# Linear attention into a gated feed-forward block: the third batch's projection and scores two slots later, a q load ahead of k and v, and the last additions in another order

## The chip, the core and the metric

The kernel runs on one core of a Trainium2 chip. The core has a matrix engine (TensorE, PE in the profile; its weight loads are PEld), a vector engine (VectorE, DVE), an engine for activations (ScalarE, ACT), a general one (GpSimd, POOL) and one that issues transfers (SyncE, SP). Sixteen DMA engines move data; loads are issued from POOL, stores and transposing transfers from SP. The metric is the device time of one launch in microseconds (us).

## The reference

Eight batches (b) with eight heads each. E and F project 1024 positions to 64 before the attention, and the result goes through a gated feed-forward block:

```python
k_proj = einsum('ks,bhsd->bhkd', E, k)          # k, v: 8 x 8 x 1024 x 64; E, F: 64 x 1024
v_proj = einsum('ks,bhsd->bhkd', F, v)
scores = (1 / sqrt(64)) * q @ k_proj.T          # per batch and head: 1024 x 64
attn   = exp(scores - max) / (sum(...) + 1e-9)
x      = (attn @ v_proj) laid out as 8192 x 512
g      = x @ w_gate                             # 512 x 1536
out    = (g * sigmoid(g) * (x @ w_val)) @ w_out # 1536 x 512
```

Inputs and output are float32; the kernel multiplies in bf16.

## The kernel before

**Chunks and iterations.** The 8192 rows are cut into 16 chunks of 512 (c; two to a batch, and chunk c belongs to batch c // 2). The feed-forward block takes 12 iterations to a chunk, one for each 128 of the 1536 columns: `f_g` (four matmuls with w_gate, then a tanh on ACT) and `f_v` (four with w_val, then two products on DVE, which make the bf16 tile hT). There are 192 iterations t.

**Slots.** Everything that the attention needs is put into numbered slots, two to an iteration. In iteration t the program order is: `f_g`, slot 2t, `f_v`, pieces of the output product of the chunk before (`f_m`), slot 2t + 1. Each engine works through its own instructions in this program order and waits at the first that isn't ready. The slots are written out by hand in `place(b)` and the lines behind it; in a slot, loads come first.

**Batches.** The text counts batches from 0, so the third batch is b == 2. For a batch the slots hold:

- `load_k`, `load_v`, and `load_q` twice (the two halves of 512 rows): DMAs from POOL's queue that convert float32 to bf16.
- `u_KV` (L162): sixteen matmuls in which k with E and v with F alternate; they use different halves of the array. ACT copies the k part (L170), DVE the v part into block-diagonal tiles (L174, L175).
- `u_KT` (L263): four matmuls that turn the projected k; DVE copies the result into block-diagonal tiles (L275, L276).
- `u_TD` (L331): a transposing DMA from SP's queue that turns one half of q into qTd.
- `u_S` (L353), eight of them: four matmuls of qTd with the projected k, an exponential on ACT; `u_R` one slot later sums and inverts on DVE; `u_N` (L383) multiplies on POOL and writes AAd.
- `u_AD` (L338): a transposing DMA from SP that turns AAd into AT; it waits for the four `u_N` of its half.
- `u_PV` (L410), eight: one matmul each of AT with the projected v; ACT copies the result to xT, which `f_g` and `f_v` of the chunk read.

Batch 1's slots: scores at 35 to 38 and 41 to 44, transpositions of weights at 41 and 47, products with v at 44, 45, 46, 46 and 66 to 69. POOL also computes sums of hT (L547, two to an iteration in the second half of a chunk) and sums for the output (L583, L594).

**The output product** of a chunk is made with fewer multiplications from sums and differences of quarters (a Strassen-like scheme with seven products m). For each half p of the rows, x holds products 3 and 5, 4 and 2; z holds 1 and 7, and 6. For the last chunk `f_m_last` does this without a next chunk to hide behind. Its products come in the order 3, 6, 4, 5 and 2, then 7, then 1. ACT copies x (`m_34`: xs; `m_52`: into ysb), POOL adds xs's halves into tt, and DVE does the rest. Products 7 and 1 of the same p use the same bank, so 1 has to wait until the addition behind 7 has read it. The four stores go out from SP (p = 0) and ACT (p = 1).

Of the kernel before, what the change touches and what calls it, by code (L numbers as in the profile page):

```python
# [10 lines left out]
ALU = mybir.AluOpType  # L11
# [27 lines left out]
def kernel(  # L39
# [19 lines left out]
    nc = tc.nc  # L59
# [450 lines left out]
    def rows_of(c):  # L510
        b, ch = divmod(c, CH)
        return out[b * S : (b + 1) * S, :].rearrange("(p c j) d -> p c j d", c=CH, j=4)[:, ch]
# [41 lines left out]
    def m_mm(c, p, m, ps, start=False):  # L554

        for f in range(HF):
            if m == 3:
                lhsT = hT[c][:, f, p * P : (p + 1) * P]
            elif m == 4:
                lhsT = hT[c][:, HF + f, HT + p * P : HT + (p + 1) * P]  # L560
            else:
                lhsT = hs[c, m][:, f, p * P : (p + 1) * P]
            rhs = {2: wo[:, f, 0:HC], 5: wo[:, HF + f, HC:DM]}.get(m)
            nc.tensor.matmul(  # L564
                out=ps,
                lhsT=lhsT,
                rhs=ws[m][:, f, :] if rhs is None else rhs,
                start=(start and f == 0),
                stop=(f == HF - 1),
                skip_group_check=True,  # L570
            )

    xx, zz, tt, yo = {}, {}, {}, {}

    def m_bank(at):
        return bank(at, [P, 2, HC], FP32, "yps")

    def m_34(c, p):

        xs = d_pool.tile([P, 2, HC], FP32, name="xs", tag="d")  # L580
        nc.scalar.copy(out=xs[:], in_=xx[c, p][:])  # L581
        t = tt[c, p] = d_pool.tile([P, 2, HC], FP32, name="tt", tag="t")
        nc.gpsimd.tensor_tensor(out=t[:, 0], in0=xs[:, 0], in1=xs[:, 1], op=ALU.add)  # L583

    def m_52(c, p):

        ysb = yo[c, p] = y_pool.tile([P, 4, HC], FP32, name="ysb", tag="ysb")
        nc.scalar.copy(out=ysb[:, 1:3], in_=xx.pop((c, p))[:])  # L588
# [27 lines left out]
    def f_m_last(c):  # L616

        xx[c, 0], xx[c, 1] = m_bank("y"), m_bank("g")
        z6 = m_bank("a")
        z1 = [m_bank("av"[p]) for p in range(2)]  # L620
        for p in range(2):
            m_mm(c, p, 3, xx[c, p][:, 0], start=True)
        for p in range(2):
            m_mm(c, p, 6, z6[:, p], start=(p == 0))
        for p in range(2):
            m_mm(c, p, 4, xx[c, p][:, 1])
            m_34(c, p)
        for p in range(2):
            m_mm(c, p, 5, xx[c, p][:, 0])
            m_mm(c, p, 2, xx[c, p][:, 1])  # L630
            m_52(c, p)
            d, ysb = tt[c, p], yo[c, p]
            nc.vector.tensor_tensor(out=d[:, 1], in0=d[:, 0], in1=ysb[:, 2], op=ALU.subtract)
            nc.vector.tensor_tensor(out=d[:, 0], in0=d[:, 0], in1=ysb[:, 1], op=ALU.subtract)
            nc.vector.tensor_tensor(out=d[:, 1], in0=d[:, 1], in1=z6[:, p], op=ALU.add)
        for x in (1, 0):
            for p in range(2):
                m_mm(c, p, (7, 1)[x], z1[p][:, 0], start=(x == 1))
                ysb = yo[c, p]
                nc.vector.tensor_tensor(out=ysb[:, 3 * x], in0=tt[c, p][:, x], in1=z1[p][:, 0], op=ALU.add)  # L640
                (nc.sync, nc.scalar)[p].dma_start(
                    out=rows_of(c)[:, p + 2 * x, :], in_=ysb[:, 2 * x : 2 * x + 2].rearrange("p x d -> p (x d)")
                )


    slots = defaultdict(list)

    def put(s, fn, *a):
        slots[s].append((fn, a))

    def place(b):
        s0 = 48 * (b - 1)
        if b == 1:
            put(22, u_TD, 1, 0)
            put(29, u_K1, 1)
            put(32, u_KT, 1)
            put(40, u_V1, 1)
            sa = (35, 36, 37, 38, 41, 42, 43, 44)
            put(41, u_AD, 1, 0)
            put(30, u_TD, 1, 1)  # L660
            put(47, u_AD, 1, 1)
            sp = (44, 45, 46, 46, 66, 67, 68, 69)
        else:
            put(s0 + (8 if b == 2 else 0), u_KV, b)
            put(s0 + (11 if b == 2 else 3), u_KT, b)
            o = 14 if b == 2 else 6
            put(s0 + (9 if b == 2 else -6), u_TD, b, 0)
            put(s0 + (11 if b == 2 else -4), u_TD, b, 1)
            sa = [s0 + o + 3 * j for j in range(NJ)]
            put(sa[3] + 4, u_AD, b, 0)  # L670
            put(sa[7] + 4, u_AD, b, 1)
            sp = [s0 + i for i in (39, 41, 43, 45, 57, 59, 61, 63)]
        for j in range(NJ):
            put(sa[j], u_S, b, j)
            put(sa[j] + 1, u_R, b, j)
            put(sa[j] + 1, u_N, b, j)
        for i in range(8):
            put(sp[i], u_PV, b, i // 4, i % 4)
# [5 lines left out]
    with tc.manual_schedule():  # L684
# [3 lines left out]
        for i in range(2):  # L688
            nc.scalar.dma_start(
                out=kraw[i][:],  # L690
                in_=k[0, 2 * i : 2 * i + 2].rearrange("h (p j) d -> p h (j d)", j=NJ),
# [123 lines left out]
        for b in range(1, B):  # L815
            place(b)
        for b in range(2, B):
            s0 = 48 * (b - 1) - (20 if b == 3 else 24)
            at = (43, 43, 44, 45) if b == 2 else (s0, s0 + 2, s0 + 4, s0 + 6)
            put(at[0], load_k, b)  # L820
            put(at[1], load_v, b)
            put(at[2], load_q, b, 0)
            put(at[3], load_q, b, 1)
# [25 lines left out]
        for t in range(NIT):  # L849
            c, f = divmod(t, NFT)  # L850
# [5 lines left out]
            for fn, *a in late.pop(t, ()):  # L856
                fn(*a)
            run_slot(2 * t + 1)
        f_m_last(NC - 1)
        assert not slots and not late  # L860

# [28 lines left out]
```

## Time and profile before

| | |
|---|---|
| median of 3 runs | 554.34 us (554.24 to 554.39) |
| the profiled execution | 554.06 us; its span, first to last instruction, 552.3 us |
| granted clock of TensorE | 1.00 throughout |
| TensorE busy | 537.3 us (97%) |
| VectorE, GpSimd, ScalarE busy | 414.1 (75%), 294.5 (53%), 233.3 us (42%) |
| read from and written to HBM | 60.29 and 16.78 MB |

Times in the profile count from the first instruction. A row of the timeline has start, duration, engine, line, operation, out<-in, shape and count; in brackets is how long the engine was idle before it, and what ended that wait. Matmuls are pipelined: they overlap, and the distance between the starts of two is what one costs. Idle time of an engine other than the one that sets the time costs nothing by itself. A DMA's landing is when its last data has arrived.

### The profile page before, as it was taken

Reading aid. Unit: us, or ns where it says so; the run is one execution under the profiler, and the core shown is the slowest. Engines: PE = TensorE matmul, PEld = TensorE weight load, DVE = VectorE, ACT = ScalarE, POOL = GpSimd, SP = SyncE. Lnnn points to the kernel's source line nnn. Section 1 sums busy time; section 2 is a strip of 40 time slices with the busy share of each in tenths; the row PEclk is TensorE's granted clock in tenths of the full one; section 3 lists DMA queues with packets and bytes.
Section 4 is the critical chain, followed back from the end, with each engine's and each line's share of the span. In section 5 each row is a group of like instructions: output and inputs, shape, how many; then the busy total and the mean of one; then the engine's idle time right before and its main releaser. Section 6 shows DMA issues by size and latency. Waiting matters only on the chain. (4 is left out here: it accounts for less than half of the span.)

```text
span 552.3 us, 9270 instructions
## 1 busy us (share of the span) xinstructions
PE 537.3 (97%) x3438; PEld 317.9 (58%) x3500; DVE 414.1 (75%) x699; ACT 233.3 (42%) x416; POOL 294.5 (53%) x364
## 2 busy tenths in 40 slices
PE   7999999999999999999999999999999999999996
PEld 4654545566565655566556655566656565555565
DVE  3787896878597875979579785788859786676883
ACT  3564453353445333443425434344244533433331
POOL 7851493467617934377534855268461763526171
PEclk9999999999999999999999999999999999999999
DMA  9999969929932598038941299214990212110013
GB/s 205 192 197 190 162 142 194 160 72 139 211 76 73 104 189 170 1 77 145 206 108 39 64 170 195 71 39 92 179 209 17 74 47 72 39 40 31 8 39 115
DMA packets 111630, 62.87 MB, mean 114 GB/s; under 512 B 65888, under 2 KB 102752, under 8 KB 111584
## 3 DMA queue, kind: packets, MB, share of 16 engines
q0 software_dynamic: 43952, 29.49, 37.5%
q1 hardware_dynamic: 66800, 31.20, 25.4%
q10 hardware_dynamic: 832, 1.57, 0.9%
q8 instruction: 27, 0.44, 0.3%
q14 instruction: 19, 0.16, 0.1%
HBM read 60.29 MB, written 16.78 MB: 140 GB/s over the span
## 5 line engine op out<-in xcount | busy, mean ns | idle before, releaser
L462 PE MATMUL vps<-xT,wv 128*128 128x512 bf16 (+1 forms) x759 | 195.0, 377 | 2.5 <-DMA wv<-in_moe_w_val_dram 0.8
L462 PE MATMUL gps<-xT,wg 128*128 128x512 bf16 (+1 forms) x729 | 191.6, 377 | 1.9
L474 ACT ACTIVATE th<-gps 128x512 f32<-128x512 f32 x191 | 114.1, 598 | 164.7 <-PE gps L462 153.9
L481 DVE SCALAR_TENSOR_TENSOR s<-th,gps 128x512 f32<-128x512 f32 x191 | 129.2, 676 | 67.5 <-ACT th L474 66.2
L547 POOL TENSOR_TENSOR hs<-hT 128x256 bf16<-128x256 bf16 x180 | 120.6, 691 | 57.9 <-DVE hT L486 57.2
L486 DVE SCALAR_TENSOR_TENSOR hT<-s,vps 128x512 bf16<-128x512 f32 x192 | 132.1, 688 | 20.4 <-PE gps L462 0.5
L462 PEld LDWEIGHTS <-wv 128*128 128x128 bf16 x776 | 73.9, 98 | 84.3 <-issue 3.0
L564 PEld LDWEIGHTS <-hs 128*128 128x128 bf16 x900 | 88.0, 98 | 36.7 <-issue 3.3
L462 PEld LDWEIGHTS <-wg 128*128 128x128 bf16 x776 | 74.1, 98 | 55.9 <-issue 0.6
L383 POOL TENSOR_TENSOR AAd<-ee,rr 128x512 bf16<-128x512 f32 x56 | 58.4, 1043 | 55.7 <-issue 33.6
L594 POOL TENSOR_TENSOR tt<-tt,ysb 128x512 f32<-128x512 f32 x28 | 35.5, 1268 | 71.7 <-DVE tt L593 71.7
L564 PE MATMUL yps<-ws,hs 128*128 128x256 bf16 x540 | 68.6, 272 | 1.5 <-DVE ysb L640 1.2
L583 POOL TENSOR_TENSOR tt<-xs 128x256 f32<-128x256 f32 x30 | 29.4, 981 | 51.3 <-ACT xs L581 51.2
L150 ACT CAST xT<-pv 128x512 bf16<-128x512 f32 (+1 forms) x63 | 36.4, 581 | 46.3 <-PE pv L410 44.3
L368 DVE TENSOR_REDUCE zz<-ee 128x8 f32<-128x512 f32 x64 | 43.3, 677 | 11.1 <-ACT ee L357 11.0
L564 PE MATMUL yps<-ws,hT 128*128 128x256 bf16 x360 | 48.8, 273 | 0.0
L564 PE MATMUL yps<-wo,hs 128*128 128x256 bf16 x360 | 48.6, 273 | 0.1
L547 DVE TENSOR_TENSOR hs<-hT 128x1536 bf16<-128x1536 bf16 (+1 forms) x49 | 46.1, 946 | 0.1
L357 ACT ACTIVATE ee<-sc 128x512 f32<-128x512 f32 x64 | 38.1, 598 | 18.5 <-PE sc L353 16.1
L564 PEld LDWEIGHTS <-hT 128*128 128x128 bf16 x360 | 35.2, 98 | 16.0
L581 ACT COPY xs<-yps 128x512 f32<-128x512 f32 x30 | 17.6, 585 | 30.6 <-PE yps L564 30.5
L588 ACT COPY ysb<-yps 128x512 f32<-128x512 f32 x30 | 17.6, 585 | 24.9 <-PE yps L564 21.6
(100 smaller groups left out, 318.0 us busy)
## 6 DMA issues: line engine op xcount, KB each, us to landing
out_dram<-ysb SPq DMA_DIRECT2D x28, 512.0 KB, 2.7
qb<-in_q_dram POOLq DMA_DIRECT2D x14, 512.0 KB, 18.1
kb<-in_k_dram POOLq DMA_DIRECT2D x7, 1024.0 KB, 9.9
vb<-in_v_dram POOLq DMA_DIRECT2D x7, 1024.0 KB, 14.8
wo<-in_moe_w_out_dram POOLq DMA_DIRECT2D x2, 768.0 KB, 21.4
out_dram<-ysb SPq DMA_DIRECT2D x6, 256.0 KB, 2.2
kraw<-in_k_dram ACTq DMA_DIRECT2D x2, 512.0 KB, 4.8
qb<-in_q_dram POOLq DMA_DIRECT2D x4, 256.0 KB, 7.9
```

Of the source, the lines that this page charges most:

```text
L150: (nc.scalar.copy if eng is nc.scalar else eng.tensor_copy)(out=out, in_=in_)
L357: nc.scalar.activation(out=e[:].rearrange("p h j k -> p (h j k)"), in_=ps[:].rearrange("p a k -> p (a k)"), func=AF.Exp, scale=scale,)
L368: nc.vector.reduce_sum(out=z[:], in_=e[:], axis=AX.X)
L383: eng.tensor_tensor(out=a.rearrange("p j h k -> p h j k"), in0=ee.pop((b, u))[:], in1=rr.pop((b, u))[:].unsqueeze(3).to_broadcast([P, 4, 2 ...
L462: nc.tensor.matmul(out=ps[:, ts], lhsT=(wg, wv)[w][:, kt, f * P : (f + 1) * P], rhs=x[:, kt, ts], start=(kt == 0), stop=(kt == NKT - 1),)
L474: nc.scalar.activation(out=th[:], in_=ps[:], func=AF.Tanh, scale=0.5)
L481: nc.vector.scalar_tensor_tensor(out=s1[:], in0=th[:], scalar=1.0, in1=g[:], op0=ALU.add, op1=ALU.mult)
L486: nc.vector.scalar_tensor_tensor(out=hT[c][:, f, :], in0=s1[:], scalar=0.5, in1=ps[:], op0=ALU.mult, op1=ALU.mult)
L547: eng.tensor_tensor(out=hs[c, m][:, fs, :], in0=quarter(hT[c], *a)[:, fs], in1=quarter(hT[c], *b)[:, fs], op=op,)
L564: nc.tensor.matmul(out=ps, lhsT=lhsT, rhs=ws[m][:, f, :] if rhs is None else rhs, start=(start and f == 0), stop=(f == HF - 1), skip_group ...
L583: nc.gpsimd.tensor_tensor(out=t[:, 0], in0=xs[:, 0], in1=xs[:, 1], op=ALU.add)
L594: nc.gpsimd.tensor_tensor(out=t[:], in0=t[:], in1=yo[c, p][:, 1:3], op=ALU.subtract)
```

## The change

Three things are edited, and a small helper is added. For the third batch (b == 2; s0 is 48): `u_KV` from slot 56 to 58, `u_KT` from 59 to 61, the eight score units from 62, 65, ... to 64, 67, ..., and with them their `u_R`, `u_N`, and the two `u_AD` (75 to 77, 87 to 89). Its two `u_TD` stay at 57 and 59, its products with v at 87 to 93 and 105 to 111. Its loads: k from 43 to 42, v stays at 43, the first half of q from 44 to 40, the second stays at 45. At the end, the additions of z6 come first and are added to tt's first half into its second; the last subtraction for p = 1 moves behind the first two additions to ysb.

```diff
+        add, sub = ALU.add, ALU.subtract
+        def step(o, i0, i1, op):
+            nc.vector.tensor_tensor(out=o, in0=i0, in1=i1, op=op)
+        for p in range(2):
+            step(tt[c, p][:, 1], tt[c, p][:, 0], z6[:, p], add)
         for p in range(2):
             m_mm(c, p, 5, xx[c, p][:, 0])
             m_mm(c, p, 2, xx[c, p][:, 1])
             m_52(c, p)
-            d, ysb = tt[c, p], yo[c, p]
-            nc.vector.tensor_tensor(out=d[:, 1], in0=d[:, 0], in1=ysb[:, 2], op=ALU.subtract)
-            nc.vector.tensor_tensor(out=d[:, 0], in0=d[:, 0], in1=ysb[:, 1], op=ALU.subtract)
-            nc.vector.tensor_tensor(out=d[:, 1], in0=d[:, 1], in1=z6[:, p], op=ALU.add)
+        d, ysb = [tt[c, p] for p in range(2)], [yo[c, p] for p in range(2)]
+        step(d[0][:, 1], d[0][:, 1], ysb[0][:, 2], sub)
+        step(d[0][:, 0], d[0][:, 0], ysb[0][:, 1], sub)
+        step(d[1][:, 1], d[1][:, 1], ysb[1][:, 2], sub)
         for x in (1, 0):
             for p in range(2):
                 m_mm(c, p, (7, 1)[x], z1[p][:, 0], start=(x == 1))
-                ysb = yo[c, p]
-                nc.vector.tensor_tensor(out=ysb[:, 3 * x], in0=tt[c, p][:, x], in1=z1[p][:, 0], op=ALU.add)
+                step(ysb[p][:, 3 * x], d[p][:, x], z1[p][:, 0], add)
...
+            if x:
+                step(d[1][:, 0], d[1][:, 0], ysb[1][:, 1], sub)
...
-            put(s0 + (8 if b == 2 else 0), u_KV, b)
-            put(s0 + (11 if b == 2 else 3), u_KT, b)
-            o = 14 if b == 2 else 6
+            put(s0 + (10 if b == 2 else 0), u_KV, b)
+            put(s0 + (13 if b == 2 else 3), u_KT, b)
+            o = 16 if b == 2 else 6
...
-            at = (43, 43, 44, 45) if b == 2 else (s0, s0 + 2, s0 + 4, s0 + 6)
+            at = (42, 43, 40, 45) if b == 2 else (s0, s0 + 2, s0 + 4, s0 + 6)
```

In the order in which POOL gets them, the loads of batch 2 were k, v, one multiplication, first q, a multiplication and two sums, second q. Now the first q stands directly behind the multiplication of slot 39; then come two sums, k, a multiplication, two sums, v, two multiplications, two sums and the second q. SP's order is the same in both.

More of the change, by code (lines that the diff above doesn't have):

```diff
@@ L638, in f_m_last @@
                 m_mm(c, p, (7, 1)[x], z1[p][:, 0], start=(x == 1))
-                ysb = yo[c, p]
-                nc.vector.tensor_tensor(out=ysb[:, 3 * x], in0=tt[c, p][:, x], in1=z1[p][:, 0], op=ALU.add)
+                step(ysb[p][:, 3 * x], d[p][:, x], z1[p][:, 0], add)
                 (nc.sync, nc.scalar)[p].dma_start(
-                    out=rows_of(c)[:, p + 2 * x, :], in_=ysb[:, 2 * x : 2 * x + 2].rearrange("p x d -> p (x d)")
+                    out=rows_of(c)[:, p + 2 * x, :], in_=ysb[p][:, 2 * x : 2 * x + 2].rearrange("p x d -> p (x d)")
                 )
+            if x:
+                step(d[1][:, 0], d[1][:, 0], ysb[1][:, 1], sub)
     slots = defaultdict(list)
```

## The prediction

> **What bounds the kernel now.** I read the busy share of each engine first (PE 97% of a 552.3 us span, DVE 75%, ACT 42%, POOL 53%, all matmuls at clock 1.00), then the busy times by stretches of 14 us, then PE's own waits, then the rows around each wait. TensorE sets the time: in nearly every stretch it is busy 13.8 to 13.95 us of 14, so an edit counts only if it takes away or adds idle time of PE. Three of the stretches below are short of that, and all three are places that the change touches (columns: window, its length, then busy us and instruction count of PE, PEld, DVE, ACT and POOL, PE clock, DMA share, GB/s; the third line is an ordinary stretch).
>
> ```profile
> 84.00:98.00 14.00, 13.02 (x82) 7.31 (x82) 9.43 (x14) 4.14 (x7) 3.35 (x4) 1.00 1.25 193
> 98.00:112.00 14.00, 13.54 (x88) 7.79 (x88) 11.11 (x21) 6.43 (x12) 8.31 (x11) 1.00 0.92 140
> 112.00:126.00 14.00, 13.89 (x94) 8.54 (x95) 11.15 (x20) 6.90 (x13) 9.20 (x12) 1.00 0.30 76
> 532.00:546.00 14.00, 13.42 (x106) 10.27 (x105) 8.77 (x17) 4.12 (x7) 7.08 (x9) 1.00 0.10 39
> ```
>
> PE's rows in time show the first two holes: batch 2's projection begins with k at 92.06 and stands until v has landed, and batch 2's first scores come 0.57 us late because the transposed q is not there.
>
> ```profile
> 92.06 0.40 PE L162 MATMUL kvp<-kb,ET 128*64 128x512 bf16 x1
> 93.33 0.38 PE L162 MATMUL kvp<-vb,FT 128*64 128x512 bf16 x1 [0.87 <-DMA vb<-in_v_dram]
> ...
> 102.22 1.03 PE L462 MATMUL gps<-xT,wg 128*128 128x512 bf16 x4
> 103.65 0.40 PE L353 MATMUL sc<-BD,qTd 128*128 128x128 bf16 x4 [0.41 <-DMA qTd<-qb]
> ```
>
> At the end a chain of DVE additions makes PE wait. PE may overwrite the first bank only after the addition at 546.26 has read it; six additions stand ahead of that one.
>
> ```profile
> 544.00 0.43 DVE L633 TENSOR_TENSOR tt<-tt,ysb 128x256 f32<-128x256 f32 x1 [3.97 <-ACT ysb L588]
> 544.47 0.42 DVE L634 TENSOR_TENSOR tt<-tt,ysb 128x256 f32<-128x256 f32 x1
> 544.81 0.41 DVE L635 TENSOR_TENSOR tt<-tt,yps 128x256 f32<-128x256 f32 x1
> 545.14 0.42 DVE L633 TENSOR_TENSOR tt<-tt,ysb 128x256 f32<-128x256 f32 x1
> 545.59 0.42 DVE L634 TENSOR_TENSOR tt<-tt,ysb 128x256 f32<-128x256 f32 x1
> 545.93 0.41 DVE L635 TENSOR_TENSOR tt<-tt,yps 128x256 f32<-128x256 f32 x1
> 546.26 0.75 DVE L640 TENSOR_TENSOR ysb<-tt,yps 128x256 f32<-128x256 f32 x2
> ...
> 546.73 1.47 PE L564 MATMUL yps<-ws,hs 128*128 128x256 bf16 x12 [1.18 <-DVE ysb L640]
> ```
>
> Last, where the q load will stand. POOL finishes its fourth normalisation of batch 1 at 70.64; SP then issues the transposition of that batch's first weights, and PE reads the result in the first PV product at 75.53.
>
> ```profile
> 69.59 1.05 POOL L383 TENSOR_TENSOR AAd<-ee,rr 128x512 bf16<-128x512 f32 x1
> 71.70 1.94 POOL L547 TENSOR_TENSOR hs<-hT 128x256 bf16<-128x256 bf16 x2 [1.06 <-DVE hT L486]
> ...
> 70.67 1.93 SPq L338 DMA_TRANSPOSE AT<-AAd  x1
> 75.03 0.33 SPq L508 DMA_DIRECT2D out_dram<-ysb  x1
> ...
> 75.53 0.38 PE L410 MATMUL pv<-AT,BDV 128*128 128x512 bf16 x1
> ```
>
> The tile view gives that transposition 4.2 us from issue to landing, so it lands at 74.9: 0.6 us to spare.
>
> **The change part by part.** No instruction's work is added or taken away; DVE has two additions of the same 128x256 form in place of two others. So all the cost is in waits. Times below are of the profiled execution: 554.06 us, which is its span of 552.3 and 1.8 us around it. The median of the runs shown is 554.34, 0.28 us above it; I add the sum to the median.
>
> *Projection two slots later: -1.25 us.* The sixteen projection matmuls of batch 2 go from 92.06 to 94.84 (start of the first to start of the last, 2.78 us); those of batch 3, which wait for nothing, from 149.75 to 151.28 (1.53). The difference, 1.25, is the wait. In the new place the projection follows one more f_v (0.86), the two f_m pieces of that iteration (twelve matmuls, 96.03 to 97.34: 1.3) and one f_g (0.86): f_g ended at 91.96, and 91.96 + 3.02 = 94.98. In the new order of loads q (0.5 MB) comes first: its packets come at full rate some 2.6 us after issue, as k's did (issued 76.70, full rate from 79.3), so at 73.3; q took 4.3 us of the queue in the trace (v landed at 77.64 + 15.7 = 93.3, q at 79.52 + 18.1 = 97.6), k and v 14 us (79.3 to 93.3). v then lands at about 73.3 + 4.3 + 14 = 91.6, 3 us before it is wanted. If that cover fails, each us that v is later than 95 is a us.
>
> *Scores two slots later and q earlier: -0.57 us.* gps started at 102.22 and takes 0.86 in steady state (108.01 to 108.87), so the scores could start at 103.08; they started at 103.65. In the new order q lands at about 78; its transposition stands on SP's queue behind the one of batch 1's second weights (issued 84.76, issue lasts 6.32, landed 15.8 us later, 100.6, beside the loads). The loads drain at about 91.6 + 4.0 (the second q: 97.6 to 82.72 + 18.9 = 101.6) = 95.6, not 101.6, so that transposition should land before 99 and the next about 3 us later, 102; the scores are due at 103.08 - 1.25 + 2.39 (one iteration, 99.83 to 102.22) = 104.2, later still with the stall below. Nothing is left of the wait; cover 2 to 4 us.
>
> *End in another order: -0.9 us.* Two additions with z6 now come before the ACT copies and run in DVE's idle time (3.97 us before 544.00; POOL's two sums, 541.48 to 542.89, are there). Then: first subtraction 544.00, or 543.6 when ACT's copy of 543.55 is what it waits for; second 0.34 to 0.47 later; third waits for ACT's second copy (544.27 + 0.58 = 544.85), so 544.92; then the addition that frees PE at 545.3 instead of 546.26, ending at 545.7. PE's last twelve matmuls move from 546.73 to about 545.75, and everything behind them (0.85 to the next addition, the second, two output DMAs) moves with them: -1.0. The eighth addition now stands between the two pairs, 545.95 to 546.4, before PE's product is there at 546.6: hidden. If what held the first DVE operation until 544.00 is POOL and not ACT, one addition fewer stands ahead of the first bank's and the gain is one pitch, 0.33. I take -0.9, nearer the end that ACT's rows give; bounds -1.0 and -0.33.
>
> *The first half of q at slot 40: +1.7 us.* On POOL its 0.94 us of issue fills the 1.06 us gap before 71.70, so nothing behind it moves. k's issue now comes at 73.64 in front of one normalisation (73.60 to 74.58) and two sums; v stays at 77.6, and the last normalisation of batch 1 is not later. On the DMA engines it is not hidden. It is issued at 70.64, the moment at which the transposition is issued. No row of before has a load starting into a transposition, so I bound it: from below 0 (the landing may slip by the 0.6 spare; a gain is excluded, PE arrives at 75.53 by its own work), from above the transposition that ran beside loads throughout, 15.8 us to landing: 70.67 + 15.8 - 75.53 = 10.9. Between them: alone the transposition moves some 840 packets a us (1675 in the 2 us from 72); beside a q load the two queues take turns, packet for packet, 240 each a us:
>
> ```profile
> q0 software_dynamic: 962, 0.49, 87.7%
> q1 hardware_dynamic: 963, 0.25, 46.6%
> ...
> q1 hardware_dynamic: 1675, 0.43, 116.4%
> ```
>
> (queue, packets, MB, share of the engines; the first two lines are 93 to 97 us, the third is 72 to 74.) By 73.3, when q's packets come at full rate, 1195 of 2080 are done; 885 at 240 a us are 3.7 us instead of 1.1, so landing slips by 2.6 and PE waits 2.0; with the packets that the first, slow q ones displace 2.3. The nearest row is milder: the transposition issued at 97.69 ran beside the last 4 us of a q load and landed after 5.9 us, 1.7 over 4.2, which would be a wait of 1.1. I take the middle of 1.1 and 2.3.
>
> [...] The turns are in the trace (962 against 963), and they speak against loading q here. [...]
>
> *At no cost.* Weights of batch 2: their first transposition moves from 120.97 to about 123.5, now beside k of batch 3 (issued 125.47). Most of its packets go before k's; PV needs it at 137.75, so it has 14 us. Beside loads throughout it would take 14.7 (the one at 136.21) and cost 0.7; bound 0 to 0.7, I take 0. DVE's four block-diagonal copies end 0.3 us before the scores, as before (102.76 against 103.08): 0, bound 0.3. SP's queue keeps its order, so no DMA is moved past another there.
>
> Sum: -1.25 - 0.57 - 0.9 + 1.7 = -1.02. 554.34 - 1.02 = 553.3.
>
> **The rivals.** *The load is not felt* (0 to 0.6 us of wait): q's packets come slowly at first, as k's (51 in 77 to 79.3), and most of the transposition slips through. Against it: 885 packets are left at 73.3. Sum -1.25 - 0.57 - 0.9 + 0 to 0.6: 551.6 to 552.2.
> *Slower: the collision is the larger one.* The same place, PE's wait at the first PV of batch 1. Right behind q come k and v with packets twice as large, so the transposition is never alone again; for it speaks that six transpositions beside a full queue took 14.7 to 16.4 us. Against it, those had their whole 2080 packets to move. It decides from a wait of 3.8 us on (landing at 79.4 or later): 555.45; at 6 us 557.6.
> *The waits only move, or the end does not shorten:* the score transposition is late behind its predecessor, or DVE's first operation waits for POOL. Half of the 2.72 gained is lost: -1.36 + 1.7 = +0.34, 554.7.
>
> **How the numbers follow.** Chances: forecast 0.45 (its own range, wait 1.1 to 2.3: 552.7 to 553.9), load not felt 0.2, larger collision 0.2, waits move 0.15. 0.2% of 554.34 is 1.1 us, about what a measurement of this kernel can tell from no change: the limits are 553.2 and 555.45. The forecast lies by the first limit, so half of it is faster; with the case of no collision 0.43. Same: the other half and the fourth case, 0.37. Slower 0.2. The range runs from the case without collision, 551.6, to just over the point at which the collision decides, 555.6; what is left out is most of the larger collision.
>
> **What the profile after would show.** Step one and two: no wait for v and none for the transposed q, the projection's sixteen matmuls in 1.5 us. End: the last twelve matmuls with a wait of 0.2 and not 1.18 us. Load: a wait of PE at the first PV of batch 1 for AT, and that transposition's time to landing 6 to 7 us. The prediction is wrong if that landing stays under 5 (then lower) or passes 9 (then higher).

## The result, and the profile after

The changed kernel takes 558.18 us in the median (557.71 to 561.31, six runs) against 554.29 for the kernel before, measured beside it (553.72 to 554.43, six runs): a ratio of 1.0084, 95% interval 1.006 to 1.0109. It is slower by 3.9 us; 553.3 was forecast, with a range up to 555.6. The three gains of the forecast came (projection, scores, end). The early q load cost several times what I had given it, and a cost behind it was missing altogether. The profiled execution is the slowest of the six: 561.31 us, span 559.5.

PE's waits, the two longest of seven (who waited, for what, us in total, times, longest): the waits for v and for the transposed q are gone, and one is there that is larger than both together. The wait of 1.2 us belongs to the start of the kernel and was there before.

```profile
PE pv L410 <- DMA AT<-AAd: 6.9, 1, 6.9
PE warm L731 <- DVE zeros L709: 1.2, 1, 1.2
```

PE's timeline of the changed kernel at that place:

```profile
75.43 0.39 PE L353 MATMUL sc<-BD,qTd 128*128 128x128 bf16 x4
82.72 0.61 PE L410 MATMUL pv<-AT,BDV 128*128 128x512 bf16 x1 [6.90 <-DMA AT<-AAd]
83.12 1.91 PE L462 MATMUL vps<-xT,wv 128*128 128x512 bf16 x4
84.83 1.91 PE L498 MATMUL yps<-wo,hT 128*128 128x512 bf16 x4
86.53 0.63 PE L410 MATMUL pv<-AT,BDV 128*128 128x512 bf16 x1
86.96 1.55 PE L462 MATMUL gps<-xT,wg 128*128 128x512 bf16 x4
88.35 0.59 PE L410 MATMUL pv<-AT,BDV 128*128 128x512 bf16 x2
88.78 1.03 PE L462 MATMUL vps<-xT,wv 128*128 128x512 bf16 x4
```

The first PV of batch 1 starts at 82.72 instead of 75.53. And the matmuls behind it are slow: four of 512 columns take 1.71 us from start to start (83.12 to 84.83), where 0.86 is usual. The busy times by stretches show the clock at half there (the column behind the five engines is PE's granted clock); whether that is the cause is tried below:

```profile
76.00:80.00 4.00, 0.00 (x0) 0.00 (x0) 3.24 (x6) 0.71 (x2) 3.98 (x5) 1.00 1.52 151
80.00:82.00 2.00, 0.00 (x0) 0.00 (x0) 0.00 (x0) 0.00 (x0) 0.62 (x1) 0.80 1.30 215
82.00:84.00 2.00, 1.28 (x4) 0.46 (x5) 0.00 (x0) 0.59 (x1) 0.00 (x0) 0.50 1.26 221
84.00:86.00 2.00, 2.00 (x6) 0.73 (x5) 0.93 (x2) 0.00 (x0) 0.16 (x1) 0.50 1.24 207
86.00:88.00 2.00, 2.00 (x6) 0.76 (x5) 1.43 (x3) 0.59 (x1) 2.00 (x3) 0.50 1.24 206
88.00:90.00 2.00, 2.00 (x11) 0.88 (x9) 0.72 (x2) 1.45 (x3) 1.72 (x2) 1.00 1.25 208
```

While PE stands still its clock falls to half (at 81.2), and it stays there until 88. Of POOL and SP, the issues of the q load and of the transposition stand 0.1 us apart, and the issue of the transposition now takes 3.62 us (before 1.93):

```profile
70.68 0.94 POOL L116 DMA_DIRECT2D qb<-in_q_dram  x1
...
70.77 3.62 SPq L338 DMA_TRANSPOSE AT<-AAd  x1
```

It lands after 11.9 us, and before after 4.2.

The projection no longer waits (its sixteen matmuls start from 104.89 to 106.43, 1.54 us), and the scores start at 114.01, 0.86 behind the f_g of 113.15: no wait. Both are seen here (first and last k and v matmul, f_g, scores):

```profile
104.89 0.40 PE L162 MATMUL kvp<-kb,ET 128*64 128x512 bf16 x1
104.89 0.40 PE L162 MATMUL kvp<-vb,FT 128*64 128x512 bf16 x1
...
106.42 0.38 PE L162 MATMUL kvp<-kb,ET 128*64 128x512 bf16 x1
106.43 0.38 PE L162 MATMUL kvp<-vb,FT 128*64 128x512 bf16 x1
...
113.15 1.03 PE L462 MATMUL gps<-xT,wg 128*128 128x512 bf16 x4
114.01 0.39 PE L353 MATMUL sc<-BD,qTd 128*128 128x128 bf16 x4
```

At the end, the additions of z6 lie in time that DVE had free, and four additions instead of seven stand between ACT's first copy and the last twelve matmuls, which now wait 0.15 us (they need the first of the two at 553.19):

```profile
550.21 0.42 DVE L631 TENSOR_TENSOR tt<-tt,yps 128x256 f32<-128x256 f32 x1 [2.21 <-POOL tt L583]
550.89 0.42 DVE L631 TENSOR_TENSOR tt<-tt,yps 128x256 f32<-128x256 f32 x1 [0.26 <-POOL tt L583]
551.54 0.76 DVE L631 TENSOR_TENSOR tt<-tt,ysb 128x256 f32<-128x256 f32 x2 [0.23 <-ACT ysb L588]
552.85 0.43 DVE L631 TENSOR_TENSOR tt<-tt,ysb 128x256 f32<-128x256 f32 x1 [0.55 <-ACT ysb L588]
553.19 0.77 DVE L631 TENSOR_TENSOR ysb<-tt,yps 128x256 f32<-128x256 f32 x2
...
552.03 1.47 PE L564 MATMUL yps<-ws,hs 128*128 128x256 bf16 x12
553.66 1.47 PE L564 MATMUL yps<-ws,hs 128*128 128x256 bf16 x12 [0.15 <-DVE ysb L631]
```

The two profiled executions differ by 7.2 us in span, and the parts can be read off. PE is 0.1 us later before the place (scores at 75.43 and not 75.31). The first PV is 7.1 later than that (82.72 less 75.53, less 0.1). The slow stretch from the first PV to the next iteration's f_v takes 6.06 us (82.72 to 88.78) and took 3.46 (75.53 to 78.99): +2.6. The projection gains 1.24, the scores 0.57, the end 1.02 (552.03 to 553.66 is 1.63; 544.08 to 546.73 was 2.65). Together 7.0. The median is 3.1 us below this execution. The mean granted clock is 0.993 in the two longest runs and 0.995 or 0.996 in the other four, so the fall of the clock may be shorter there as well as the wait; of those runs no rows are on record, so how the 3.1 us are shared is not shown.

### The profile page after: what moved, and what is told of

Same layout as the page of the kernel before. It is cut to its first block, busy times and chain, and to the rows that moved or that the text cites. A ratio compares the mean times of both kernels' runs of the same rounds, so it can differ in the third digit from the quotient of the medians.

```text
span 559.5 us, 9333 instructions
## 1 busy us (share of the span) xinstructions
PE 544.2 (97%) x3500; PEld 318.5 (57%) x3500; DVE 415.2 (74%) x699; ACT 233.1 (42%) x416; POOL 296.1 (53%) x364
## 4 chain that ended last, share of the span: by engine, by line
PE 80%; DVE 11%; DMA 4%; issue 1%; POOL 1%; ACT 1%; DVEq 0%; POOLq 0%; ACTq 0%
PE gps L462 26%; PE vps L462 25%; PE yps L564 22%; DVE s L481 3%; DVE hs L547 2%; PE pv L410 2%; DMA wv<-in_moe_w_val_dram 2%; DMA AT<-AAd 2%; DVE hT L486 2%; PE kvp L162 2%; PE sc L353 2%; PE yps L498 1%; DVE zz L368 1%; DVE BD L276 1%; DVE BD L275 1%
## 5 line engine op out<-in xcount | busy, mean ns | idle before, releaser
L462 PE MATMUL vps<-xT,wv 128*128 128x512 bf16 (+1 forms) x776 | 198.4, 378 | 0.7 <-DMA wv<-in_moe_w_val_dram 0.7
L462 PE MATMUL gps<-xT,wg 128*128 128x512 bf16 (+1 forms) x772 | 197.0, 378 | 0.0
L368 DVE TENSOR_REDUCE zz<-ee 128x8 f32<-128x512 f32 x64 | 43.3, 677 | 12.3 <-ACT ee L357 12.2
L410 PE MATMUL pv<-AT,BDV 128*128 128x512 bf16 x60 | 22.9, 387 | 7.0 <-DMA AT<-AAd 6.9
```

Source lines behind the costliest of these rows:

```text
L368: nc.vector.reduce_sum(out=z[:], in_=e[:], axis=AX.X)
L410: nc.tensor.matmul(out=ps[:].rearrange("p (j t) -> p j t", t=P), lhsT=BDV[b % 2][:, pr, :], rhs=AT[b, ch][:, :, pr, :], start=True, stop=True,
L462: nc.tensor.matmul(out=ps[:, ts], lhsT=(wg, wv)[w][:, kt, f * P : (f + 1) * P], rhs=x[:, kt, ts], start=(kt == 0), stop=(kt == NKT - 1),)
```

## The experiments

**Theory after the result:** the whole loss is the q load at slot 40, which meets the transposition of AT, and the fall of the clock that the wait brings. **Rival:** the later projection and scores lose the time, by the order in which ACT, DVE and POOL get their work. Four kernels take the change apart.

*Only the end.* The additions as in the changed kernel, slots and loads as before:

```diff
-            put(s0 + (10 if b == 2 else 0), u_KV, b)
-            put(s0 + (13 if b == 2 else 3), u_KT, b)
-            o = 16 if b == 2 else 6
-            at = (42, 43, 40, 45) if b == 2 else (s0, s0 + 2, s0 + 4, s0 + 6)
+            put(s0 + (8 if b == 2 else 0), u_KV, b)
+            put(s0 + (11 if b == 2 else 3), u_KT, b)
+            o = 14 if b == 2 else 6
+            at = (43, 43, 44, 45) if b == 2 else (s0, s0 + 2, s0 + 4, s0 + 6)
```

> Only the new order of the additions at the end; slots and loads as before. Theory (the q load at slot 40 makes the whole loss: a wait for AT at the first PV of batch 1, and slow matmuls behind it): the last twelve matmuls start about 1.0 us earlier, -1.0 us, 553.3. Rival (the later projection and scores lose the time): the same here. If the order of the end gained nothing, 0.

Measured 553.04 against 554.23 (ratio 0.998, 95% interval 0.9968 to 0.9991): 1.2 us faster, close to the 1.0 expected.

*Only the slots* of the projection and the scores (the kernel before with):

```diff
-            put(s0 + (8 if b == 2 else 0), u_KV, b)
-            put(s0 + (11 if b == 2 else 3), u_KT, b)
-            o = 14 if b == 2 else 6
+            put(s0 + (10 if b == 2 else 0), u_KV, b)
+            put(s0 + (13 if b == 2 else 3), u_KT, b)
+            o = 16 if b == 2 else 6
```

> Only the projection, its turn and the scores of the third batch two slots later; loads and end as before. Theory: both waits of PE (for v 1.25 us, for qTd 0.57 us) are gone and nothing comes in their place: -1.8 us, 552.5. Rival (the later slots lose time in the order of ACT, DVE or POOL): slower than before, up to +4 us.

Measured 552.67 against 554.23 (0.9968, 0.9955 to 0.998): 1.6 us faster, and neither wait is left in PE's list. The rival falls: the later slots lose nothing.

*All but the loads:*

```diff
-            at = (42, 43, 40, 45) if b == 2 else (s0, s0 + 2, s0 + 4, s0 + 6)
+            at = (43, 43, 44, 45) if b == 2 else (s0, s0 + 2, s0 + 4, s0 + 6)
```

> The whole change but the loads, which stay at 43, 43, 44, 45. Theory: -1.8 for the two waits and -1.0 for the end, no wait for AT and the clock at 1.00: 551.5, faster than both. Rival: about as slow as the changed kernel, 558.

Measured 551.73 against 554.23 (0.9951, 0.9939 to 0.9964): 2.5 us faster than before, and 6.4 us faster than the changed kernel. Clock 1.00.

*Only the loads* (the kernel before with the line of loads of the changed one):

> Only the loads at 42, 43, 40, 45; slots and end as before. Theory: the wait for AT (3.5 to 7 us) and the slow matmuls behind it (2.6 us) are there, and since PE is late, the waits for v and qTd are gone (-1.8): +4.3 to +7.8 us, 558.6 to 562. Rival (the slots lose it): 552.5 to 554.5.

Measured 559.6 against 554.23 (1.009, 1.0069 to 1.0112): 5.4 us slower. PE waits for AT, which lands after 11.0 us:

```profile
PE pv L410 <- DMA AT<-AAd: 5.8, 1, 5.8
```

The line of loads is the whole loss; the two other edits, slots and end, gain 2.5 us together.

**What of the load does it?** Next, when it is issued, what follows it, and how large it is.

*One slot later:*

```diff
-            at = (42, 43, 40, 45) if b == 2 else (s0, s0 + 2, s0 + 4, s0 + 6)
+            at = (42, 43, 41, 45) if b == 2 else (s0, s0 + 2, s0 + 4, s0 + 6)
```

> The changed kernel with its early q load one slot later, at 41 and not 40: on POOL it then stands behind two sums, 3 us later, ahead of k. Theory (the load meets the transposition of AT): the transposition's packets are nearly all out when the first of q come, it lands after 4.2 to 5 us, PE does not wait, clock 1.00: 551.7 us, as with the old loads. Rival (q ahead of k and v is itself the loss): 556 or more.

Measured 551.65 against 554.12 (0.9954, 0.9941 to 0.9967): 2.5 us faster than before. The load is issued 2.9 us behind the transposition (SP's row and POOL's):

```profile
70.81 1.95 SPq L338 DMA_TRANSPOSE AT<-AAd  x1
...
73.74 0.94 POOL L116 DMA_DIRECT2D qb<-in_q_dram  x1
```

The DMA queues from 71 to 75 us (queue, packets, MB, share): in this kernel all 2080 packets of the transposition are out before the first of q, and it lands after 4.2 us.

```profile
q1 hardware_dynamic: 2080, 0.52, 70.5%
```

In the changed kernel, in the same 4 us, only half of them are, though only 55 of q's have come:

```profile
q1 hardware_dynamic: 1013, 0.26, 80.5%
q0 software_dynamic: 55, 0.03, 5.5%
```

So q ahead of k is harmless, and the distance of 0.1 us from the transposition is not. This kernel and the one with the old loads are the fastest of the study; between them (551.65 and 551.73) there is no difference to be told. In its profiled execution the kernel with the old loads still waits 0.3 us for the transposed q, and this one does not; that is all that moving q ahead brought, and it does not show in the time.

*Nothing behind q for a while* (k and v at slot 47):

```diff
-            at = (42, 43, 40, 45) if b == 2 else (s0, s0 + 2, s0 + 4, s0 + 6)
+            at = (47, 47, 40, 45) if b == 2 else (s0, s0 + 2, s0 + 4, s0 + 6)
```

> The changed kernel with k and v moved from 42 and 43 to 47, so that nothing follows q for some 10 us. Taking turns with all that is loaded (q, then k): the transposition should land sooner than the 11.9 us of the changed kernel, at 7 to 9 us, PE waits 2 to 4 us, and 554 to 556 us. Issued together is what matters: landing 11 to 12 us as before, wait 6 to 7, 558 to 561 us (more if v is late for the projection).

The transposition landed after 11.8 us and PE waited 6.6, as in the changed kernel (11.9 and 6.9): k and v behind q are not needed for it. The time, 568.28, is longer than expected, since v now is late for the projection too (a wait of 6.0 us; the mean granted clock of the profiled execution is 0.986, in the changed kernel 0.993).

*Half of q at slot 40*, the other half at 44, k and v at 47:

```diff
+            if b == 2:
+                put(40, load_q, b, 0, (0, 4), (0, 4))
+                put(44, load_q, b, 0, (0, 4), (4, 8))
+            else:
+                put(at[2], load_q, b, 0)
-            put(at[2], load_q, b, 0)
```

> As the kernel with k and v at 47, and only half of that q load (four of eight heads) at slot 40, the other half at 44. Taking turns by packets: half of the packets, half of the delay: landing 6 to 8 us. Issued together is what matters, whatever the size: landing 10 us or more.

Landing after 7.7 us, wait 2.6: 3.5 us over the undisturbed 4.2, where a whole q costs 7.6. That speaks for a delay that goes with the size of the load, as taking turns would have it, and against "whatever the size". It is one profiled execution, though, and with a whole q issued just as close the landing varies: 9.1 to 12.2 us in five kernels, so 4.9 to 8.0 over the undisturbed. (565.83 us in all, again with v late, by 6.2.)

*Some distance.* One sum of hT on POOL, or two, which only repeat a result, ahead of the load:

```diff
+        def hold(n):
+            for _ in range(n):
+                h_sum(1, 5, 1, 2)
+        put(39, hold, 1)        # the second kernel: 2
```

> The changed kernel with one sum of hT on POOL (0.7 us, repeated with the same result) in front of the early q load, so that it is issued 0.7 us behind the transposition of AT and not 0.1. If two issues at the same moment hold each other up: the hold-up is gone, and only taking turns is left: 1200 to 1500 of 2080 packets out before q's come, landing 6 to 8 us, wait 1 to 3 us, 553 to 555. If any load within the transposition's time does the same: landing 11 to 12 us, 558.

The load was issued 0.5 us behind the transposition, and the landing came after 7.4 us (wait 2.4), where taking turns was to have it; the median, 555.26, is 0.3 us above what that theory said. But the packets are not as it said (1200 to 1500 out before q's come), and tell something that neither theory had. From 71 to 75 us all of the data is out, 2048 packets of 256 bytes:

```profile
q1 hardware_dynamic: 2048, 0.52, 71.6%
q0 software_dynamic: 42, 0.02, 14.1%
```

but the last 32 come between 76.4 and 78.5, in the midst of q's packets. They carry 0.00 MB, and the landing, at 78.2, falls among them, so I read them as the reports of the end:

```profile
q0 software_dynamic: 654, 0.34, 132.2%
q1 hardware_dynamic: 32, 0.00, 2.1%
```

The data was out by 75 and the landing was at 78.2; what held the reports in between the rows do not tell (q's packets came slowly at first: 223 from 75 to 76.4, 654 from 76.4 to 78.5). So this transposition was late beside a load that began before its last reports (7.4 us to landing and not 4.2), though its data was out by 75 as without the load. The landing in this view is then, as I read it, the moment of the report, and not, as the section on the profile before has it, the arrival of the last data.

> The same with two such sums, 1.4 us behind the transposition. Issued together: landing 5 to 6.5 us, wait 0 to 1.5, 551.7 to 553.2. Any load: a landing of 9 us or more, 556 or more.

With two sums, 1.3 us behind, it is the same: 2048 packets by 75 us, landing after 7.9, wait 2.8. Here I was wrong: the landing does not come earlier with the distance, until the load begins behind the reports as in the kernel with slot 41. The medians are 555.26 (ratio to before 1.0022, 1.0008 to 1.0036) and 556.16 (1.0023, 1.0008 to 1.0038). The second kernel's runs spread from 551.63 to 556.63; the lowest is the time of a kernel without the collision, so perhaps the reports slipped through in that run, which nothing on record shows.

**Is the slow stretch behind the wait the clock, by idleness?** Matmuls whose result is not used, in front of the first PV of batch 1 in the changed kernel:

```diff
+        def fill(n):
+            ps = bank("v", [P, CW], FP32, "fill")
+            for _ in range(n):
+                nc.tensor.matmul(
+                    out=ps[:], lhsT=wo[:, 0, 0:P], rhs=wo[:, 1, :], start=True, stop=True
+                )
...
+        if b == 1:
+            put(44, fill, 16)        # the second kernel: 32
```

> The changed kernel with sixteen matmuls of 512 columns (3.5 us), whose result is not used, put in front of the first PV of batch 1, so that PE stands idle for 3.5 us at most instead of 7. Theory (the clock falls because PE stands idle, and the matmuls behind the wait cost 2.6 us more for it): clock 1.00 behind the wait, 555.6 us. Rival (these matmuls are slow because of the transfers beside them): still slow, 558 us.

Measured 556.95 (ratio to before 1.0067, 1.0044 to 1.0089), 1.2 us less than the changed kernel though sixteen matmuls were added; the runs of the two overlap (556.03 to 560.47 and 557.71 to 561.31), so the time alone decides nothing. In the profiled execution, the longest of the six, 3.6 us of idleness were left, and the clock fell again, for 3.4 us (83.0 to 86.4, worked out from the spacing of PE's matmuls; the f_v behind the PV took 1.70 us) and not 6.8. The direction is the theory's, the size is not, since PE still stood idle.

> The changed kernel with 32 unused matmuls (6.9 us) in front of the first PV of batch 1, so that PE hardly stands idle though AT is as late. Clock falls for idleness: clock 1.00 behind the PV, the next four vps matmuls 0.86 us apart as a group and not 1.7, and 551.7 + 6.9 = 558.6 us in every run. Slow for the transfers beside them: they stay at 1.7 us, 561.

Measured 558.74 (558.66 to 559.17), as expected. AT is late here too (landing after 9.1 us), but PE is busy, the clock stays at 1.00 in every stretch from 76 to 90 (two of them are shown), and the f_v behind the PV takes 0.86 us (82.97 to 83.83):

```profile
82.00:84.00 2.00, 2.00 (x11) 0.87 (x9) 0.00 (x0) 0.58 (x1) 0.00 (x0) 1.00 1.24 207
84.00:86.00 2.00, 2.00 (x11) 0.89 (x10) 1.97 (x3) 0.61 (x2) 1.20 (x1) 1.00 1.24 206
...
82.75 0.38 PE L410 MATMUL pv<-AT,BDV 128*128 128x512 bf16 x1
82.97 1.03 PE L462 MATMUL vps<-xT,wv 128*128 128x512 bf16 x4
83.83 1.03 PE L498 MATMUL yps<-wo,hT 128*128 128x512 bf16 x4
```

As many transfers run beside them (from 84 to 86 the DMA share is 1.24 in both kernels). The slow stretch is the clock, and here it falls because PE stands still: from 84 to 86 it was 0.50 behind 6.9 us of idleness and 1.00 without. Shorter waits were enough too: in the two kernels with some distance it was at half for 3.4 us behind waits of 2.4 and 2.8 us. The kernel with one sum of distance:

```profile
78.23 0.39 PE L410 MATMUL pv<-AT,BDV 128*128 128x512 bf16 x1 [2.43 <-DMA AT<-AAd]
...
78.00:80.00 2.00, 1.76 (x8) 0.78 (x9) 1.79 (x5) 0.59 (x1) 1.98 (x3) 0.88 1.22 176
80.00:82.00 2.00, 2.00 (x6) 0.70 (x5) 2.00 (x2) 0.52 (x1) 2.00 (x4) 0.50 1.18 250
```

What stays open: in the changed kernel the transposition is held up even before the first packet of q is seen (500 of its packets from 71 to 73.3, 12 more up to 74; before 1195 and 1773, and with the load at 41, where the transposition is issued at the same moment, 1065 and 1655). This early hold-up is gone with 0.5 us between the two (1078 by 73.3). What they share at 0.1 us was not tried, nor why the landing varies so much among the five kernels that issue a whole q so close (9.1 to 12.2 us).

## Why the prediction was wrong

- *Projection two slots later, -1.25:* right. 1.54 us from first to last start, v lands at 93.8 (77.61 + 16.2; 91.6 was forecast), 11 us before it is wanted since PE is late. Where PE is not late, with the load at 41, it lands at 92.6 and PE has no wait for it, so the cover was there; with the slots alone both waits are gone too.
- *Scores, -0.57:* right; the slots alone, both terms, gave 1.6 of 1.82.
- *End in another order, -0.9:* right, and a little above its upper bound of 1.0; 1.02 in the trace, 1.2 in the run of the end alone. DVE's first subtraction came right behind ACT's copy (551.54, copy to 551.51), as the upper bound had it.
- *The first half of q at slot 40, +1.7:* the step that failed. It measured +9.7 in the profiled execution (7.1 of wait, 2.6 of clock), and 6.5 in the median (558.18 less the 551.7 without the collision). The place, the taking of turns and the side effects on POOL were as told: k issued at 73.70, v at 77.61. Three parts of the sum were wrong. First, "By 73.3, when q's packets come at full rate, 1195 of 2080 are done": there were 500. I took the undisturbed row for the time before q's packets show, and the load issued at the same moment disturbed the transposition earlier than that. And the turns I then counted were slower: from 75 to 80 us the two queues move 887 and 1007 packets, some 190 each a us and not 240. Second, the sum ends with the last packet at the full rate of the turns. Here 2020 of the 2080 packets were out by 80 (1013 and 1007), and the landing came at 82.7: the last 60 took 2.7 us, and not the 0.25 that 240 a us would give. Third, the wait was taken as the whole price. Behind this wait of 6.9 us the clock was at half for 6.8 us, 5.3 of them with PE at work, which I had no row for and did not bound.
- *"The nearest row is milder":* the transposition that ran beside the end of a q load (5.9 us) was the wrong neighbour. The near ones were those with a load beside them from the start, at 14.7 to 15.8 us: 11.9 lies nearer to these. Taking the middle between my own two estimates left out the upper bound of 10.9.
- *Chances:* the rival that came, "the larger collision", was named at its place with 3.8 us as the point from which it decides, and had 0.2; its price lacked the clock. The reason it was given, that k and v behind q would feed it, is refuted (11.8 us without them).

## What to carry to other kernels

Look at which transposing transfer is in flight, and how much time it has to spare, before a load is moved ahead; a load beside it slowed its packets here (1007 in the 5 us from 75, against 1675 in 2 us alone), and where its data was out as early as without a load it still landed after 7.4 and 7.9 us and not 4.2. A gap of 3 us in the queue (here one slot, two sums of POOL) was worth 6.5 us in this kernel, and gaps of 0.5 and 1.3 us 2.9 and 2.0. Where PE will wait for 2.4 us or more, the shortest wait behind which the clock fell here, put the halved clock behind the wait into the price: 2.6 us behind the wait of 6.9. Waits of 1.2 us, as in the kernel before, left the clock at 1.00; between the two nothing was tried.

## What the runs showed that I had not expected

- Data out is not landed: with the load 0.5 to 1.3 us behind, the 2048 data packets were out by 75 us as without a load, and the landing was at 78.2 and 78.6, 3 us later.
- The clock's fall had one of two lengths in the four kernels for which it was taken: 3.4 us behind waits of 2.4, 2.8 and 3.6 us, 6.8 us behind the wait of 6.9. It can begin after the wait is over (with one sum of distance the wait ended at 78.2, and the clock was at half from 79.5 to 82.95).
- The same binary differs from run to run where the two transfers meet: 551.63 to 556.63 with two sums of distance. Three of the kernels without the collision stay within 0.8 us. The spread alone does not prove the collision: the kernel with only the end has one run at 554.73, 1.4 us above its next, and the kernel before one at 556.47, 1.8 above its next.
